# The second product of a two-layer mixture's last two token sets by Strassen's algorithm, its weights' forms made during the first layer

## Chip, cores and metric

The kernel runs on one core of a Trainium2 chip. The metric is the device time of one execution in microseconds: a median of runs, and one execution with a hardware profile. TensorE (PE) multiplies, VectorE (DVE), ScalarE (ACT) and GpSimd (POOL) do the rest, and SyncE (SP) issues the DMAs.

## The reference

Three parts in fp32, one after the other (2304 tokens, D = 512):

```python
q_s = softmax(q, over head_dim); k_s = softmax(k, over seq)
x = q_s @ (k_s.T @ v)                        # linear attention, 4 batches x 8 heads
h = x @ w_in                                 # 512 -> 2048
x = (h * clip(h + 3, 0, 6) / 6) @ w_out      # 2048 -> 512
p = domain_probs / sum(domain_probs)
for e in range(4):                           # experts, F = 1024 each
    out += p[:, e] * (relu(x @ w1[e]) @ w2[e])
```

## The kernel before

All matrices are kept as two parts, hi and lo, in the format fp32r, and each product is three matmuls: hi x hi, hi x lo and lo x hi. A matmul has a stationary tile of 128x128, loaded by a weight load of its own, and up to 512 moving columns.

**First layer** ("steps", lines 576 to 578 and 619): tokens in six blocks of 384, the 2048 inner columns in 16 chunks. A step is one chunk of one block: 12 matmuls for h, the gate (L589 on ScalarE, L592 on VectorE, L598 on ScalarE, then the low half on VectorE or GpSimd), and 12 matmuls of the second product into four PSUM banks. `PASSES1` lists which chunks run over which blocks in one pass; at the end of each pass the banks of a block are added into `acc` (L657 to L661). The weights come as 64-bit words and are unpacked on VectorE and ScalarE (L524 to L544) one chunk after another.

**Second layer** ("units", here sets): three sets of 768 tokens. Within a set the 4 x 1024 inner columns are 16 pairs of 256 columns, and two pairs are a group; `UNITS`, `NPR`, `GROUP`. The first product of a pair is a 2x2 block product (token halves, inner halves, contraction halves) by Strassen's algorithm in Winograd's form: seven products instead of eight, in the order 1, 7, 5, 6, 4, 3, 2, each 6 matmuls of 384 columns (L847). The x forms (`x_forms`) are made once a set, from sums of token and contraction blocks; the weights' forms (`w_first`) in the first set, and stored to a DRAM scratch `wd`, from which the later sets read them (L742). After the products, additions out of PSUM (L294) give the four blocks of h; `finish` applies relu and splits them into hi and lo: L924 on ScalarE, L931 on VectorE. The second product (`y_ops`, L969) is plain: for each of six token tiles and both pairs, 6 matmuls of 512 columns, whose stationary side is h; VectorE multiplies the sum by the token's share p and adds it to `acc` (L1007). Its weights are split in the first set, stored to `vd` and read back by the later sets (L798).

TensorE's order is fixed by the program: the products of one group alternate with the second-product tiles of the group before it (`tail`). For the other engines a list scheduler (`Plan.order`) sets the order ahead of time from costs written in `dve`, `act`, `pool_`, `pe` and `hop`, from due times worked back from TensorE's, and from "places": numbered buffers that an operation takes and gives back (w: weight tiles, g: tiles of h, t: temporaries, x: x forms, raw2, wtmp, xt: staging). `rather_pool` and `either` let the planner choose between GpSimd and VectorE. Each engine, SyncE too, then runs its own list strictly in order.

## Time and profile before

| | us |
|---|---|
| median of 3 runs (1259.03 to 1263.07) | 1261.53 |
| the profiled execution | 1259.79 |
| its span, first to last instruction | 1257.8 |
| TensorE busy in it | 1220.6 (97%) |
| attention and first layer, up to | about 498 |
| first set of the second layer, up to | about 742 |

The span leaves out what lies before the first and behind the last instruction. TensorE's recorded matmuls overlap, so the time that one of them takes of the engine is read from the distance of their starts and not from their durations. An engine's idle time is given with what ended it.

### The profile page before, as it was taken

The numbers are of one execution on the slowest core, as the hardware profiler recorded it, in microseconds if no ns is written. First come the engines' busy times: TensorE is split into PE (matmuls) and PEld (weight loads), VectorE is DVE, ScalarE is ACT, GpSimd is POOL, SyncE is SP. The second block draws the span as 40 slices with busy tenths as digits, with TensorE's granted clock in tenths as the row PEclk, the third lists the DMA queues.
The fourth block names the chain that finished last, engine by engine and source line by source line (L and its number), as shares of the span: only waits on it lengthen the run. The fifth ranks groups of instructions, "written<-read, shape, count | busy, mean of one in ns | idle before, by whom it ended". The sixth has DMA issues, their size and how long they took to land.

```text
span 1257.8 us, 17479 instructions
## 1 busy us (share of the span) xinstructions
PE 1220.6 (97%) x6432; PEld 1128.2 (90%) x6432; DVE 690.4 (55%) x1149; ACT 489.2 (39%) x985; POOL 334.2 (27%) x328
## 2 busy tenths in 40 slices
PE   4889999999999999999999999999999999999998
PEld 3678999999999999988888888888888888888887
DVE  8889641686365634655555684444444544444443
ACT  5667432553244334544444432222222322222221
POOL 5656222431015104667776710000000000000000
PEclk8889999999999999999999999999999999999999
DMA  8343200222013004787777656555555665555551
GB/s 290 109 147 127 68 17 1 65 70 68 1 35 109 1 1 156 270 285 252 251 251 251 226 193 209 184 184 184 184 186 185 216 205 186 185 184 184 185 167 51
DMA packets 99909, 192.59 MB, mean 153 GB/s; under 512 B 11249, under 2 KB 11249, under 8 KB 99825
## 3 DMA queue, kind: packets, MB, share of 16 engines
q1 hardware_dynamic: 99824, 191.49, 45.7%
q8 instruction: 51, 0.84, 0.3%
q14 instruction: 34, 0.27, 0.1%
HBM read 140.59 MB, written 50.86 MB: 152 GB/s over the span
## 4 chain that ended last, share of the span: by engine, by line
PE 87%; DVE 7%; issue 2%; POOL 1%; DMA 1%; ACT 0%; SPq 0%; DVEq 0%; POOLq 0%; ACTq 0%
PE ps L969 31%; PE ps L847 27%; PE ps L619 14%; PE ps L576 4%; PE ps L578 4%; PE ps L577 4%; DVE x L294 1%; PE ps L378 1%; DVE st L530 1%; PE ps L472 1%; DMA vs<-in_v_dram 1%; DMA qs<-in_q_dram 1%; PE ps L433 1%; DVE g L931 1%; DVE g L294 0%
## 5 line engine op out<-in xcount | busy, mean ns | idle before, releaser
L969 PE MATMUL ps<-w,g 128*128 128x512 f32 x1728 | 446.3, 394 | 2.5 <-ACT g L924 2.5
L847 PE MATMUL ps<-x,w 128*128 128x384 f32 x2016 | 396.5, 335 | 0.0
L847 PEld LDWEIGHTS ps<-x,w 128*128 128x128 f32 x2016 | 359.5, 188 | 25.2
L969 PEld LDWEIGHTS ps<-w,g 128*128 128x128 f32 x1728 | 320.4, 188 | 54.0 <-ACT g L924 3.0
L619 PE MATMUL ps<-g,w 128*128 128x384 f32 x1152 | 224.2, 340 | 5.7 <-ACT g L598 5.7
L294 POOL TENSOR_TENSOR w<-st,w 128x256 fp32r<-128x256 f32 (+1 forms) x160 | 155.4, 992 | 209.9 <-ACT w L544 87.6
L619 PEld LDWEIGHTS ps<-g,w 128*128 128x128 f32 x1152 | 201.7, 189 | 8.9 <-ACT g L598 6.7
L924 ACT ACTIVATE g<-t 128x384 fp32r<-128x384 f32 x192 | 100.8, 525 | 230.6 <-DVE t L294 224.0
L1007 DVE SCALAR_TENSOR_TENSOR acc<-ps,pt,acc 128x512 f32<-128x512 f32 x126 | 94.6, 751 | 167.0 <-PE ps L969 166.9
L855 ACT ACTIVATE t<-ps 128x384 f32<-128x384 f32 x192 | 94.3, 492 | 233.9 <-PE ps L847 233.9
L931 DVE SCALAR_TENSOR_TENSOR g<-t,g 128x384 fp32r<-128x384 f32 x192 | 124.2, 648 | 64.2 <-ACT g L924 64.1
L576 PE MATMUL ps<-x,w 128*128 128x384 f32 x384 | 130.5, 340 | 0.0
L577 PE MATMUL ps<-x,w 128*128 128x384 f32 x384 | 129.3, 337 | 1.1 <-DVE x L479 1.1
L578 PE MATMUL ps<-x,w 128*128 128x384 f32 x384 | 129.0, 336 | 0.0
L592 DVE SCALAR_TENSOR_TENSOR r<-r,ps 128x384 f32<-128x384 f32 x96 | 53.0, 552 | 127.9 <-ACT r L589 127.3
L589 ACT ACTIVATE r<-ps,three 128x384 f32<-128x384 f32 x96 | 55.6, 579 | 143.2 <-PE ps L578 143.2
L294 DVE TENSOR_TENSOR t<-ps,t 128x384 f32<-128x384 f32 x144 | 79.7, 554 | 40.7 <-PE ps L847 38.0
L294 DVE TENSOR_TENSOR t<-t 128x384 f32<-128x384 f32 x94 | 57.3, 610 | 70.6 <-ACT t L855 70.2
L577 PEld LDWEIGHTS ps<-x,w 128*128 128x128 f32 x384 | 72.7, 189 | 2.1 <-DVE x L479 2.0
L576 PEld LDWEIGHTS ps<-x,w 128*128 128x128 f32 x384 | 72.7, 189 | 0.8 <-ACT x L475 0.5
L578 PEld LDWEIGHTS ps<-x,w 128*128 128x128 f32 x384 | 72.7, 189 | 0.0
L598 ACT ACTIVATE g<-r 128x384 fp32r<-128x384 f32 x96 | 50.3, 524 | 52.5 <-DVE r L592 52.1
(104 smaller groups left out, 834.5 us busy)
## 6 DMA issues: line engine op xcount, KB each, us to landing
w<-wd SPq DMA_DIRECT2D x224, 256.0 KB, 4.3
w<-vd SPq DMA_DIRECT2D x128, 256.0 KB, 2.8
wd<-w SPq DMA_DIRECT2D x112, 256.0 KB, 2.5
st<-in_w_dram SPq DMA_DIRECT2D x64, 256.0 KB, 3.6
vd<-w SPq DMA_DIRECT2D x64, 256.0 KB, 3.9
st<-in_w_dram SPq DMA_DIRECT2D x30, 512.0 KB, 3.7
out_dram<-acc SPq DMA_DIRECT2D x18, 256.0 KB, 2.0
vs<-in_v_dram SPq DMA_DIRECT2D x12, 322.5 KB, 4.1
```

The lines of the kernel that those rows point to most:

```text
L294: on(o).tensor_tensor(out=out, in0=a, in1=b, op=op)
L576: nc.tensor.matmul(pst[0], lhsT=hi, rhs=a, start=(k == 0), stop=False)
L577: nc.tensor.matmul(pst[0], lhsT=hi, rhs=b, start=False, stop=False)
L578: nc.tensor.matmul(pst[0], lhsT=lo, rhs=a, start=False, stop=(k == NK - 1))
L589: nc.scalar.activation(out=pst["r"], in_=pst[0], func=AF.Relu, bias=three)
L619: nc.tensor.matmul(y, lhsT=l, rhs=r, start=(s["start"] and not low and m == 0), stop=(s["stop"] and bool(low)))
L847: nc.tensor.matmul(bank(i), lhsT=l, rhs=r, start=(opens and k == 0 and m == 0), stop=(k == 1 and m == 2), skip_group_check=not opens)
L855: nc.scalar.activation(out=t, in_=bank(i), func=AF.Copy)
L924: nc.scalar.activation(out=g[:, :n], in_=x(), func=AF.Relu)
L931: nc.vector.scalar_tensor_tensor(out=g[:, n:2 * n], in0=x(), scalar=0.0, in1=g[:, :n].bitcast(F32), op0=ALU.max, op1=ALU.subtract)
L969: nc.tensor.matmul(y, lhsT=l, rhs=rr, start=opens and x == 0, stop=closes and x == len(seq) - 1)
L1007: o1 = add({"DVE": dve(DM) + 0.05}, lambda o: nc.vector.scalar_tensor_tensor(out=a, in0=state[ti], scalar=s, in1=a, op0=ALU.mult, op1=ALU. ...
```

## The change

In the last two sets the second product becomes a Strassen product too: inner halves of a pair by output halves of 256 columns by token halves. Its left side (h) needs seven forms per pair, of which four are sums; relu stands before them, so h's blocks are first finished (`relu`, and two-operand steps with a maximum) and then summed: s1, n2, s3, s4. Each of the seven products is 6 matmuls of 256 columns for each of three token tiles and the two pairs of a group together. Products 1, 6, 7 and 4 of a tile add up in the same PSUM region, 5 and 3 in another, 2 stands alone; after each, VectorE multiplies the region by p and adds it into the block of `acc` that Winograd's scheme needs (`INTO`).

The weights' seven forms for it (`w_prepare(pr, 1)`, all 16 pairs) are made during the first layer, after the attention's memory is free, and stored to `vd`; the places for that are taken from w, g and t of the first layer. A pass more is made in the first layer. The first set keeps the plain second product (`h_ops0`, `y_ops0`, `w_second0`), and no longer stores its halves. The later sets read seven forms per pair instead of four halves. x places are lent to h and t, and one staging buffer to h. The planner's costs change: VectorE operations between SBUF tiles, GpSimd, and the way to and from SyncE.

```diff
-PASSES1 = [(0, 3, range(3)), (3, 6, range(3)), (0, 6, range(3, 6)), (6, 11, range(6)),
-           (11, 16, range(6))]
+PASSES1 = [(0, 3, range(3)), (3, 6, range(3)), (0, 6, range(3, 6)), (6, 9, range(6)), (9, 13, range(6)), (13, 16, range(6))]
...
-BLOCKS = [(0,), (1,), (2,)]
...
+ORDER2 = (5, 2, 1, 6, 3, 7, 4)
+CHAIN = {5: "x", 3: "x", 2: "b", 1: "a", 6: "a", 7: "a", 4: "a"}
+BANK2 = {"x": ((0, 0), (0, 256), (1, 0)), "b": ((2, 0), (2, 256), (1, 256)),
+         "a": ((3, 0), (3, 256), (2, 0))}
+INTO = {5: (1, 1), 2: (0, 0), 1: (0, 0), 6: (0, 1), 3: (0, 1), 7: (1, 1), 4: (1, 0)}
...
-MORE_W, MORE_G, MORE_T = 2, 4, 5
-NX, NXG = 24, 4
+MORE_W, MORE_G, MORE_T = 2, 4, 3
+RING, WAIT = 2, 2
+NX, NXG = 24, 7
...
-    return 0.27 if b == "PE" else 0.2 if a == "PE" else 1.05 if a == "SP" else 0.16
+    if b == "SP":
+        return 2.0
+    return 0.27 if b == "PE" else 0.2 if a == "PE" else 2.5 if a == "SP" else 0.16
...
+def dve2(n):
+    return 0.155 + 1.6e-3 * n
...
-    return 0.15 + 2.25e-3 * n
+    return 0.2 + 2.4e-3 * n
...
-    vd = dram.tile([NPR, 2, 2, P, DM], F32, name="vd")
+    vd = dram.tile([NPR, 7, P, DM], F32, name="vd")
...
-    XT = [s[:, 768 * i:768 * (i + 1)] for s in ST for i in range(2)]
+    XT = [ST[0][:, 768 * i:768 * (i + 1)] for i in range(2)]
...
+    def w_prepare(pr, second):
...
+        p0, p1 = [raw2(2 * pr + f) for f in range(2)]
...
+            o = temps[i] = load("wtmp", rather_pool(half), make, ready[a] + ready[b], ("wtmp", None))
...
+        def form(i):
+            pl = w_new(store, (pr, i, second), "wr")
+            t = (pr, i, second)
+            o1 = add({"ACT": act(half)}, lambda o: nc.scalar.activation(
+                out=store[t][:, :half], in_=vals[i](), func=AF.Copy), ready[i] + [pl])
+            give = [("wtmp", temps[i])] if i in temps else []
+            o2 = add(rather_pool(half), lambda o: half_sub(
+                o, store[t][:, half:], vals[i](), store[t][:, :half]),
+                [o1] + (readers[i] if i in temps else []), None, give)
+            w_stored[t] = add({"SP": 0.9}, lambda o: nc.sync.dma_start(
+                out=(vd if second else wd)[pr, i - 1], in_=store[t].bitcast(F32)), [o2], None,
+                [("wr", pl)])
+            all_.append(o2)
...
+        form(1)
+        if second:
+            summed(7, 0, 3, ALU.subtract)
+        else:
+        form(7)
+        summed(5, 0, 1, ALU.subtract)
+        summed(6, 5, 3, ALU.subtract)
+        form(5)
+        summed(4, 2, 6, ALU.add)
+        form(6)
+        form(4)
+        form(3)
+        form(2)
+        stage2.append(add({"": 0.0}, lambda o: None, all_, None, [("raw2", p0), ("raw2", p1)]))
...
+    def w_bring(pr, second, i):
+        store, kept = (w2, vd) if second else (w1, wd)
+        pl = w_new(store, (pr, i))
+        return load("sp", {"SP": 0.9}, lambda o: nc.sync.dma_start(
+            out=store[pr, i].bitcast(F32), in_=kept[pr, i - 1]), [pl, w_stored[pr, i, second]]), pl
...
-        sts = []
-        for x, o in enumerate((o1, o2)):
-            sts.append(add({"SP": 0.9}, lambda o, x=x: nc.sync.dma_start(
-                out=vd[pr, f, x], in_=w2[pr, f, x].bitcast(F32)), [o]))
-            w_stored[pr, "v", f, x] = sts[-1]
-        stage2.append(o2)
-        return [o1, o2], pls, sts
...
-    def h_ops(pr, u, weights, last):
+    def h_ops(pr, u):
...
+        def relu(src, dep):
+            return add({"ACT": act(n)}, lambda o: nc.scalar.activation(
+                out=at(src), in_=at(src), func=AF.Relu), [dep])
...
+        def form(i, src, deps, raw, free):
...
+            o2 = add({"DVE": dve2(n)} if raw else rather_pool(n), low,
+                     [o1] + (free or []), None, [] if free is None else [("t", src)])
...
+        def make(i):
+            ld, pl = w_bring(pr, 0, i)
+            deps = [ld, xf["op", (u, i)]] + bank_free.get(BANK[i], [])
+            give = [("w", pl)]
+            if pr == NPR - 1:
+                give += [("x", pl) for pl in x_place[u, i]]
+            ops[i] = main_pe(6 * pe(n), lambda o: product(o, i), deps, None, give)
+            if i in (1, 7, 5, 6):
+                pos[i] = evict(i)
+                bank_free[BANK[i]] = [pos[i]]
+            if i == 6:
+                y0, p5, uu = pos[7], pos[5], pos[6]
+                s = add(rather_pool(n), lambda o: tt(o, at(y0), at(y0), at(p5), ALU.add), [y0, p5],
+                        None, [("t", p5)])
+                c22 = pos["c22"] = add(rather_pool(n), lambda o: tt(
+                    o, at(y0), at(y0), at(uu), ALU.add), [s, uu])
+                pos["r22"] = relu(y0, c22)
+            if i == 4:
+                uu, y0 = pos[6], pos[7]
+                c = pos["c21"] = tmp({"DVE": dve(n)}, lambda o, t: tt(
+                    o, t, bank(4), at(uu), ALU.add), [ops[4], uu])
+                bank_free[1] = [c]
+                s1 = pos["s1"] = tmp({"DVE": dve2(n)}, lambda o, t: nc.vector.scalar_tensor_tensor(
+                    out=t, in0=at(c), scalar=0.0, in1=at(y0), op0=ALU.max, op1=ALU.add),
+                    [c, pos["r22"]])
+                form(4, y0, [pos["r22"]], False, [s1])
+            if i == 3:
+                uu = pos[6]
+                c = pos["c12"] = tmp({"DVE": dve(n)}, lambda o, t: tt(
+                    o, t, bank(3), at(uu), ALU.add), [ops[3], uu])
+                bank_free[2] = [c]
+                add({"": 0.0}, lambda o: None, [c, pos["c21"], pos["c22"]], None, [("t", uu)])
+                form(5, pos["s1"], [pos["s1"]], False, None)
+                pos["l2"] = form(2, c, [c], True, None)
+            if i == 2:
+                a0, c21, c12, s1 = pos[1], pos["c21"], pos["c12"], pos["s1"]
+                c11 = add({"DVE": dve(n)}, lambda o: tt(o, at(a0), bank(2), at(a0), ALU.add),
+                          [ops[2], a0])
+                bank_free[3] = [c11]
+                r11 = relu(a0, c11)
+                n2 = tmp(either(n), lambda o, t: tt(o, t, at(a0), at(s1), ALU.subtract), [r11, s1])
+                s3 = add({"DVE": dve2(n)}, lambda o: nc.vector.scalar_tensor_tensor(
+                    out=at(c21), in0=at(c21), scalar=0.0, in1=at(a0), op0=ALU.max,
+                    op1=ALU.subtract), [r11, s1])
+                s4 = add({"DVE": dve2(n)}, lambda o: nc.vector.scalar_tensor_tensor(
+                    out=at(c12), in0=at(c12), scalar=0.0, in1=at(n2), op0=ALU.max, op1=ALU.add),
+                    [n2, pos["l2"], made[2][1]])
+                add({"": 0.0}, lambda o: None, [n2, made[5][2]], None, [("t", s1)])
+                form(1, a0, [r11], False, [n2, s3])
+                form(6, n2, [n2], False, [s4])
+                form(3, c12, [s4], False, [])
+                form(7, c21, [s3], False, [])
...
+    def y_ops(u, prs, gs, step):
...
+        def part(i, t):
...
+                opens = i in (5, 2, 1)
...
+                for pi, pr in enumerate(prs):
+                    g, ww = gs[pi][i][0], w2[pr, i]
+                    hi, lo = g[:, :n][:, c], g[:, n:2 * n][:, c]
+                    seq += [(hi, ww[:, :half]), (hi, ww[:, half:]), (lo, ww[:, :half])]
+                for x, (l, r) in enumerate(seq):
+                    nc.tensor.matmul(y, lhsT=l, rhs=r, start=clears and x == 0,
+                                     stop=x == len(seq) - 1, skip_group_check=True)
...
+                if t == 0:
+                    weights[i] = [w_bring(pr, 1, i) for pr in prs]
...
+                if i in (5, 2, 1):
+                    deps += bank2_free.get(b, []) if at == 0 else []
+                else:
+                    deps += dep[key]
+                o = main_pe(6 * pe(half), fn, deps)
+                if t == n // P - 1:
+                    o.give += [("g", gs[pi][i][3]) for pi in range(len(prs))]
+                    o.give += [("w", pl) for _, pl in weights[i]]
+                dep[key] = [evict(i, t, o)]
...
+            y = PS[4 + b][:, at:at + half]
...
+            if fresh:
+                o1 = add({"DVE": dve(half)}, lambda o: nc.vector.tensor_scalar_mul(a, y, s),
+                         [made] + norm + x_read[u, hf])
+            else:
+                o1 = add({"DVE": dve(half) + 0.03}, lambda o: nc.vector.scalar_tensor_tensor(
+                    out=a, in0=y, scalar=s, in1=a, op0=ALU.mult, op1=ALU.add), [made])
+            o1.due = made.due + made.eng["PE"] + 1.5
...
+        return [part(i, t) for i in ORDER2 for t in range(n // P)]
...
-        [("w", NW + i) for i in range(MORE_W)] + [("g", NG + i) for i in range(MORE_G)]
+        [("wr", NW + i) for i in range(MORE_W)] + [("raw2", NG + i) for i in range(MORE_G)]
+        + [("wtmp", i) for i in range(3)]
         + [("t", NT_ + i) for i in range(MORE_T)] + [("ph", 2), ("ph", 3)])
...
+    for pr in range(NPR):
+        w_prepare(pr, 1)
...
+    add({"": 0.0}, lambda o: None, stage2, None, [("g", NG + i) for i in range(MORE_G)])
+    ring = [o for s, o in zip(steps, products) if s["c"] == PASSES1[-2][0]][:1]
+    for i in range(RING):
+        o = add({"": 0.0}, lambda o: None, ring, ("w", None), (), 0.0)
+        o.give.append(("wr", o))
+    for i in range(MORE_W + RING):
+        o = add({"": 0.0}, lambda o: None, stage2, ("wr", None), (), 0.0)
+        o.give.append(("w", o))
...
-        o = load("xg", {"": 0.0}, lambda o: None, [evicted[NK - 1]], ("x", None))
+        o = load("xg", {"": 0.0}, lambda o: None, [evicted[NK - 1]], ("x", None), 0.0)
         o.give.append(("g", lambda o=o: 100 + o.place))
+    load("xg", {"": 0.0}, t_of_x, (), ("x", None), 0.0).give += [("t", 100), ("t", 101)]
...
+            slots = GROUP * len(ORDER) - WAIT
+            count = len(tail)
+            for x, pr in enumerate(group):
+                make, gs[x] = h_ops(pr, u)
+                for z, i in enumerate(ORDER):
+                    make(i)
+                    slot = x * len(ORDER) + z - WAIT + 1
+                    while slot > 0 and count - len(tail) < -(-count * slot // slots):
+                        tail.pop(0)()
...
+            tail += y_ops(u, group, gs, step)
+        if u == 0:
+            add({"": 0.0}, lambda o: None, stage0, None, [("xt", i) for i in range(2)])
+            add({"": 0.0}, g_of_stage, stage0, None, [("g", 200), ("g", 201)])
...
```

## Rows read from the trace of the kernel before

**Rows 1.** The page, part 1: span, and TensorE's busy time (instructions).

```profile
span 1257.8 us, 17479 instructions
...
PE 1220.6 (97%) x6432; PEld 1128.2 (90%) x6432; DVE 690.4 (55%) x1149; ACT 489.2 (39%) x985; POOL 334.2 (27%) x328
```

**Rows 2.** Busy time by stretch: length, each engine's us; granted clock, DMA share, GB/s.

```profile
core 0: us, PE busy (x) PEld busy (x) DVE busy (x) ACT busy (x) POOL busy (x), PEclk, DMA share, GB/s
165.00:491.30 326.30, 323.49 (x1865) 322.78 (x1864) 170.01 (x283) 130.29 (x238) 78.95 (x70) 1.00 0.12 40
541.80:741.80 200.00, 198.30 (x990) 177.98 (x988) 120.65 (x164) 96.10 (x207) 136.38 (x147) 1.00 0.71 248
...
930.40:961.70 31.30, 31.30 (x158) 28.13 (x157) 14.12 (x25) 8.14 (x16) 0.00 (x0) 1.00 0.58 187
```

**Rows 3.** Timeline of TensorE, second set: start, us, engine, line, tiles, shape, count.

```profile
900.97 1.55 PE L969 MATMUL ps<-w,g 128*128 128x512 f32 x6
902.36 1.21 PE L847 MATMUL ps<-x,w 128*128 128x384 f32 x6
903.41 1.55 PE L969 MATMUL ps<-w,g 128*128 128x512 f32 x6
```

**Rows 4.** Timelines in the attention: weight loads (PEld), and matmuls with 129 columns.

```profile
52.06 0.19 PEld L619 LDWEIGHTS ps<-g,w 128*128 128x128 f32 x1
...
52.06 0.30 PEld L619 LDWEIGHTS ps<-g,w 128*128 128x128 f32 x2
...
57.59 1.27 PE L378 MATMUL ps<-vs,acc 128*128 128x129 f32 x10
58.70 1.28 PE L378 MATMUL ps<-spare,acc 128*128 128x129 f32 x10
```

**Rows 5.** Groups by shape, VectorE, 830 to 1200: busy us, mean ns, idle before.

```profile
L931 DVE SCALAR_TENSOR_TENSOR g<-t,g 128x384 fp32r<-128x384 f32 x96 | 53.3, 555 | 34.4 <-ACT g L924 34.3
L1007 DVE SCALAR_TENSOR_TENSOR acc<-ps,pt,acc 128x512 f32<-128x512 f32 x65 | 48.8, 751 | 92.0 <-PE ps L969 92.0
L294 DVE TENSOR_TENSOR t<-ps,t 128x384 f32<-128x384 f32 x72 | 40.0, 555 | 26.2 <-PE ps L847 24.7
```

**Rows 6.** Groups by shape, VectorE, 500 to 700, where GpSimd works too.

```profile
L931 DVE SCALAR_TENSOR_TENSOR g<-t,g 128x384 fp32r<-128x384 f32 x53 | 42.5, 804 | 16.2 <-ACT g L924 16.2
```

**Rows 7.** Groups by shape, VectorE, 170 to 400: an eviction of 384 columns.

```profile
L661 DVE SCALAR_TENSOR_TENSOR acc<-ps,acc 128x384 f32<-128x384 f32 x32 | 15.6, 548 | 2.3 <-PE ps L619 2.3
```

**Rows 8.** Groups by shape, GpSimd, whole span: operations of 256 and 384 columns.

```profile
L294 POOL TENSOR_TENSOR w<-st,w 128x256 fp32r<-128x256 f32 x112 | 89.4, 826 | 91.5 <-PE ps L619 58.4 <-ACT w L764 32.6 <-DVE g L931 0.5
...
L294 POOL TENSOR_TENSOR g<-r,g 128x384 fp32r<-128x384 f32 x25 | 28.0, 1122 | 57.7 <-ACT g L598 51.3 <-PE ps L619 6.4
...
L294 POOL TENSOR_TENSOR t<-t 128x384 f32<-128x384 f32 x2 | 3.0, 1502 | 250.2 <-ACT t L855 248.7 <-DVE t L294 1.4
```

**Rows 9.** Groups by shape, ScalarE, 830 to 1200.

```profile
L924 ACT ACTIVATE g<-t 128x384 fp32r<-128x384 f32 x95 | 49.9, 525 | 136.9 <-DVE t L294 136.1 <-POOL t L294 0.8
L855 ACT ACTIVATE t<-ps 128x384 f32<-128x384 f32 x94 | 46.3, 492 | 134.8 <-PE ps L847 134.8
```

**Rows 10.** Timeline of TensorE where the second set begins.

```profile
742.56 2.08 PE L969 MATMUL ps<-w,g 128*128 128x512 f32 x6 [2.46 <-ACT g L924]
744.43 2.12 PE L847 MATMUL ps<-x,w 128*128 128x384 f32 x6
746.36 2.18 PE L969 MATMUL ps<-w,g 128*128 128x512 f32 x6
```

**Rows 11.** Groups by shape, VectorE, 700 to 745: forms of the next set.

```profile
L294 DVE TENSOR_TENSOR x<-acc,x 128x768 fp32r<-128x768 f32 x4 | 5.1, 1270 | 0.0
```

**Rows 12.** Waits of TensorE, 165 to 495: total us, times, longest.

```profile
PE ps L619 <- ACT g L598: 2.8, 2, 1.5
```

**Rows 13.** DMA issues: count, KB each, median us to landing.

```profile
w<-wd SPq DMA_DIRECT2D x224, 256.0 KB, 4.3
```

**Rows 14.** Timeline of TensorE at the end of the span.

```profile
1241.58 12.53 PE L969 MATMUL ps<-w,g 128*128 128x512 f32 x54
```

More of the change, by code (lines that the diff above doesn't have):

```diff
@@ L280, in queue, with load @@
         return in_turn.setdefault(name, [])
-    def load(name, eng, fn, deps=(), take=None):
-        o = add(eng, fn, queue(name) + list(deps), take)
+    def load(name, eng, fn, deps=(), take=None, key=None):
+        o = add(eng, fn, queue(name) + list(deps), take, (), key)
         in_turn[name] = [o]
@@ L493, in half_sub, with w_new @@
         tt(o, out, x, hi.bitcast(F32), ALU.subtract)
-    def w_new(store, key, deps=()):
+    def w_new(store, key, kind="w"):
         def new(o):
             store[key] = w_tile(o.place, "w_" + "_".join(str(x) for x in key))
-        return load("w", {"": 0.0}, new, deps, ("w", None))
+        return load(kind, {"": 0.0}, new, (), (kind, None))
     w0, w_done, w_place = {}, {}, {}
@@ L583, in h_part @@
         h_before[:] = [o0]
+        products.append(o0)
         if s["x_last"]:
@@ L704, in x_forms @@
             key = u, i
-            pls = x_place[key] = [load("form", {"": 0.0}, lambda o: None, rdy, ("x", None))
+            pls = x_place[key] = [load(
+                "form", {"": 0.0}, lambda o: None, rdy + (queue("xg") if u else []), ("x", None))
                                   for _ in range(2)]
@@ new lines, in tile_kernel, with raw0 @@
+    w1, w2 = {}, {}
+    def w_bring(pr, second, i):
[3 more added lines that the diff above has]
+            out=store[pr, i].bitcast(F32), in_=kept[pr, i - 1]), [pl, w_stored[pr, i, second]]), pl
+    w2_0 = {}
+    stage0 = []
+    def raw0(c, i):
+        ld = load("raw0", {"SP": 0.95}, lambda o: nc.sync.dma_start(
+            out=RAW2[o.place], in_=w[c][:, i * DM:(i + 1) * DM]), (), ("raw0", None))
@@ L828, in h_ops, with h_ops0 @@
+    last0 = []
+    def h_ops0(pr, u, weights, last):
         n = UNITS[u][1]
@@ L977, in emit @@
                     deps.append(o1 if low == 0 else o2)
-                if step["last"] and closes:
-                    for pr2 in prs:
-                        for f in range(2):
-                            deps += seconds[pr2, f][2]
                 o = main_pe(cnt * pe(DM), fn, deps, ("y", None) if opens else None)
@@ L1061, in tile_kernel @@
         h_part(i, s)
-    for b in range(NK):
-        add({"": 0.0}, lambda o: None, [evicted[b]], None, [("y", b)])
     for i in range(4):
         bank_free[i] = list(last1)
+        add({"": 0.0}, lambda o: None, [evicted[i]], None, [("y", i)])
+    for pr in range(NPR):
[5 more added lines that the diff above has]
+        o.give.append(("wr", o))
@@ L1073, in tile_kernel, with t_of_x, g_of_stage @@
         o.give.append(("g", lambda o=o: 100 + o.place))
-    weights, seconds = {}, {}
+    def t_of_x(o):
+        t = xp.tile([P, 768], F32, tag=f"x{o.place}", name="tx")
+        t_more[100], t_more[101] = t[:, :384], t[:, 384:]
+    load("xg", {"": 0.0}, t_of_x, (), ("x", None), 0.0).give += [("t", 100), ("t", 101)]
+    def g_of_stage(o):
+        t = wsp.tile([P, 3 * DM], F32R, tag="st1", name="gs")
+        g_more[200], g_more[201] = t[:, :768], t[:, 768:]
     tail = []
-    for blk, units in enumerate(BLOCKS):
+    for u in range(len(UNITS)):
@@ L1077, in tile_kernel @@
         for g0 in range(0, NPR, GROUP):
             group = list(range(g0, g0 + GROUP))
-            for pr in group:
-                weights[pr] = w_first(blk, pr)
-            for pr in group:
-                for f in range(2):
-                    seconds[pr, f] = w_second(blk, pr, f)
-            for u in units:
-                step = dict(first=g0 == 0, final=g0 + GROUP >= NPR, last=u == units[-1], e=g0 // NPE)
-                gs = [None, None]
-                early, late_ = y_ops(u, group, gs, seconds, step)
+            step = dict(first=g0 == 0, final=g0 + GROUP >= NPR, last=True, e=g0 // NPE)
@@ L1088, in tile_kernel @@
+            gs = [None] * GROUP
+            if u == 0:
+                firsts0 = [w_first0(pr) for pr in group]
+                seconds0 = {(pr, f): w_second0(pr, f) for pr in group for f in range(2)}
+                early, late_ = y_ops0(u, group, gs, seconds0, step)
                 for x, pr in enumerate(group):
-                    make, gs[x] = h_ops(pr, u, weights[pr], step["last"])
+                    make, gs[x] = h_ops0(pr, u, firsts0[x], True)
                     for z, i in enumerate(ORDER):
@@ L1098, in tile_kernel @@
                 tail += late_
-        if blk == 0:
-            add({"": 0.0}, lambda o: None, stage2, None, [("xt", i) for i in range(4)])
-        if blk < 2:
-            x_forms(blk + 1)
+                continue
+            slots = GROUP * len(ORDER) - WAIT
[7 more added lines that the diff above has]
+                        tail.pop(0)()
+            if not bank2_free:
+                for i in range(4):
+                    bank2_free[i] = list(last0)
+            tail += y_ops(u, group, gs, step)
+        if u == 0:
+            add({"": 0.0}, lambda o: None, stage0, None, [("xt", i) for i in range(2)])
+            add({"": 0.0}, g_of_stage, stage0, None, [("g", 200), ("g", 201)])
+        if u + 1 < len(UNITS):
+            x_forms(u + 1)
     for f in tail:
```

190 lines of the change are left out of this document (148 added, 42 removed).

## The prediction, made before the change was run

> **What bounds the kernel now.** I read the page's busy line first, then the busy time by stage, then single instructions of TensorE. TensorE is busy 97% of the span [rows 1]. By stage the reader is to see that it is the bound in every one: in the first layer (165 to 491.3 us) it loses 2.8 of 326.3 us, in the first set of the second layer (541.8 to 741.8) 1.7 of 200, and in the last two sets nothing: one group of two pairs takes 31.3 us, all of it busy, while VectorE has 14.1 and ScalarE 8.1 us of work and GpSimd none [rows 2]. So a TensorE instruction taken out of the last two sets is worth its whole spacing, as long as no other engine fills up.
>
> The spacing is read from starts, since recorded durations overlap. Six 512-column matmuls lie between 900.97 and 902.36, 1.39 us, and six of 384 columns between 902.36 and 903.41, 1.05 us [rows 3]: 0.231 and 0.175 us each. A group has 84 of the second kind (14 products of 6) and 72 of the first (6 token tiles x 2 pairs x 2 chunks x 3): 14.65 + 16.65 = 31.3 us, which is the stretch above. The account closes, so the sum below is made with these.
>
> **The second product.** 72 matmuls of 512 columns become 126 of 256 (7 forms x 3 token tiles x 6). That is 7/8 of the columns, but 54 more instructions. No fp32r matmul here has 256 columns. From below: half of the 512-column one, 0.116 us; from above: the line through 384 and 512 columns, 0.231 - 2 x 0.056 = 0.119. I take 0.117, so 14.75 us instead of 16.65: 1.9 us per group, with ends 1.65 and 2.05. Sets two and three have 8 groups each: **16 x 1.9 = 30 us** (26 to 33).
>
> This holds only while the next stationary tile is loaded behind a running matmul. Every matmul has its own load, recorded as 188 ns, more than 117. But at 52.06, where TensorE starts anew, the first load is recorded as 0.19 us and two together as 0.30, so the second starts 0.11 after the first; and in the attention, ten 129-column records with a load each take 1.11 us (57.59 to 58.70), 0.111 apiece [rows 4]. A load thus goes through in 0.11 us, just under the 0.117 that it must hide behind. The margin is thin, and that is the first rival. The Trainium skill (TensorE: Matmul & The Clock Gate, Part 3, The mechanism) says that a weight load overlaps running matmuls only in another row group; by that rule the 54 further loads of a group would each show. The trace speaks against it: 384 columns at 2.4 GHz are 0.16 us, and a shown load would make the spacing 0.27, not 0.175.
>
> **The other engines in the last two sets.** Per pair VectorE gets three additions out of PSUM at 0.555 us [rows 5], four two-operand steps between SBUF tiles and one more subtraction, which took 0.555 with GpSimd idle [rows 5] and 0.804 with it at work [rows 6]; I take 0.8, since GpSimd will work: 5.7 us, 11.4 per group. It also gets 21 evictions of 256 columns instead of 6 of 512 at 0.751 [rows 5]. At 384 columns from PSUM one took 0.548 [rows 7]; the line through both gives 0.35 at 256, and 0.548 itself is the other end. I take 0.45: 9.5 us (7 to 11.5). Together 21 of 29.4 us, 71%. The two sums for the block C22 and six low halves per pair may go to GpSimd, 16 per group at 1.12, 1.5 where VectorE competes [rows 8]: 18 to 24 us. ScalarE has 8 evictions at 0.492 and 18 steps at 0.525 [rows 9]: 13.4 us. None is full. TensorE runs in a fixed order, so what counts is whether a result comes before its turn: a group's forms are wanted only after three more products (3.1 us). The tight chain is another: tiles 1, 6, 7, 4 add up in one PSUM bank, so each must be evicted before the next is added. Between a tile's turn in 1 and in 6 lie two other tiles and at least one product, 2 x 0.70 + 1.05 = 2.45 us; drain, eviction and restart are about 0.9 (twice the eviction, an estimate), and 1.5 us are left for waiting behind another VectorE instruction of at most 1.3. In the first set's stretch, with VectorE at 60% and GpSimd at 68%, TensorE lost 1.7 in 200 us [rows 2]; at that rate the 470 us cost **+4** (0 to 10).
>
> DMA: 28 loads per group instead of 22. 187 GB/s at a share of 0.58 becomes about 252 GB/s; the first set moves 248 at 0.71 with TensorE full [rows 2]. A load lands in 4.3 us [rows 13], and 26 places hold nearly a group in advance. Nothing on the path. If that cover went, each late tile would cost up to those 4.3 us.
>
> **The first layer.** Prepared there: 16 pairs x (4 sums + 7 low halves) = 176 operations of 256 columns at 0.826 on GpSimd [rows 8], 145 us, on top of 79 of 326: 69%, what the first set has now. ScalarE gets 112 short copies, on 130 of 326 us. SyncE gets 32 loads and 112 stores; a store waits there for its low half, and the loads of the first layer's own weights stand behind it, though these run a chunk or more ahead. One pass more means 24 more evictions of 0.55 on VectorE (13 us on 170 [rows 2]). VectorE's gating step feeds TensorE here and gets slower beside a busy GpSimd. Today's waits in this layer are 2.8 us [rows 12]. Ends: -2.8 if they go, +16 if it crowds (second rival). I take **+2**. The first set's stores of the plain halves (64) fall away on SyncE, where nothing on the path waited for them: 0.
>
> The new planner costs (landing 2.5 instead of 1.05 us, VectorE and GpSimd dearer) reorder everything, the attention included. Nearer to the durations above, they might take a wait away as well as make one: **0**, from -4 to +4.
>
> **Borders.** Between sets one and two TensorE waits 2.46 us for ScalarE's g tile [rows 10]; the wait is behind VectorE, which was making the next set's x forms at 1.27 us each without a pause [rows 11]. After it six 384-column matmuls take 1.93 us, 0.32 each: the lower clock level, 1.2 GHz. Wait and slow clock cost some 4.4 us. The change leaves 16 x places instead of 20 for two sets that need 14 each, and two scratch tiles instead of four, so most forms wait for a product of the set's last pair; but they still have about seven products (15 us) each. It also costs the planner's forms more truly. Ends per border: -4.4 and +4.4; I take **0** in sum. At the end, 54 matmuls run after the last product with no gap [rows 14]; afterwards 21 tiles run there, the first of which need the forms of the last pair: **+1** (0 to 3).
>
> **Sum.** -30 + 4 + 2 + 0 + 0 + 1 = -23 us. The profiled execution took 1259.79 us, 2 us over its span, and lies 1.7 us under the median of 1261.53. 1259.8 - 23 = 1236.8 there; against the median, 1238.5.
>
> **Rivals.**
> 1. The load is the bound. If loads came only every 0.188 us, as recorded, a group's second product would take 126 x 0.188 = 23.7 us, 7 more than now: 16 x 7 = +113, 1374 us. It decides from a spacing of 16.65 / 126 = 0.132 on. Against it: 0.11 in [rows 4]; for it: that the trace shows no fp32r matmul under 384 columns. Chance 0.03. In a second form the load shows at every matmul that is added: 54 x 0.11 [rows 4] - 1.9 = 4 us a group, +64, 1327; it needs a spacing that 384 columns don't have [rows 3]. Chance 0.02. The skill's rule above is this form.
> 2. The preparation crowds the first layer: if each of some 78 steps (24 matmuls, 4.2 us) after 165 us waits 0.2 us longer, 16 us go, 1254. For it: gate and low half share VectorE with evictions; against: two PSUM places more let products run ahead. 0.12.
> 3. It ends slower because VectorE becomes the bound of sets two and three. If GpSimd's 16 operations fall to VectorE at 0.8 [rows 6], it has 21 + 12.8 = 33.8 us a group, 2.5 over the 31.3 of now: 16 x 2.5 = +40, 1302. It decides where VectorE's work passes 31.3 us a group. For it: GpSimd is slow and the planner gives VectorE what GpSimd can't start in time; against: GpSimd idles there now. 0.07.
> 4. It does not do what it says: the planned order does not fit the real times, waits in the chain of four take about 1.4 us a group, and all is eaten: 1261. 0.08.
>
> **How the numbers follow.** The forecast, with its own ends 1222 to 1252, gets 0.68. Low end: 33 us, no waits, first layer's waits gone. High end: 26 us, 10 for waits in groups, a few in the first layer. The range goes on to 1258, to take in rival 2. A measurement tells about 0.3% (4 us) from no change. Faster: 0.68 + 0.12 = 0.80; same 0.08; slower 0.05 + 0.07 = 0.12.
>
> **What would show it.** In the changed kernel's timeline six 256-column matmuls should start 0.70 us apart, and a group should take 29.4 to 29.8 us with TensorE busy throughout; VectorE should be at 70 to 80% there and GpSimd above 50%. The first layer should end where it ends now, within 4 us. Wrong would be: spacing above 0.132, TensorE waits on the evictions of the second product, long waits for the gate in the first layer, or several us at both borders.

## The result and the profile after

The changed kernel takes 1242.59 us (median of 4 runs, 1241.78 to 1242.94), the kernel before 1260.28 in the runs beside it: a ratio of 0.9857, 95% interval 0.9835 to 0.9879, 17.7 us less. The forecast was 1238.5 us and 23 us less, with a range from 1222 to 1258. The profiled execution, the slowest of the four, has a span of 1241.2 us, 16.6 under that of before.

The page's first part, and the busy time by stretch (length, each engine's us, granted clock, DMA share, GB/s), as [rows 1] and [rows 2] have them for before:

```profile
PE 1200.1 (97%) x7296; PEld 1151.6 (93%) x7296; DVE 877.5 (71%) x1482; ACT 595.4 (48%) x1257; POOL 665.4 (54%) x659
...
164.00:507.00 343.00, 339.49 (x1935) 334.48 (x1934) 225.26 (x343) 170.24 (x361) 209.70 (x225) 1.00 0.45 154
541.80:741.80 200.00, 200.00 (x999) 179.88 (x998) 124.58 (x187) 96.40 (x214) 115.02 (x124) 1.00 0.54 185
858.20:887.90 29.70, 29.70 (x211) 29.52 (x210) 21.78 (x41) 12.69 (x27) 13.79 (x13) 1.00 0.79 249
```

The reader is to see that TensorE is still the bound, that a group now takes 29.7 us instead of 31.3, and that it is paid for with VectorE (14.1 to 21.8 us a group) and GpSimd (0 to 13.8). TensorE's timeline in a group (start, us, line, shape, count), beside [rows 3]:

```profile
845.66 1.21 PE L933 MATMUL ps<-x,w 128*128 128x384 f32 x6
846.71 1.59 PE L1249 MATMUL ps<-w,g 128*128 128x256 f32 x12
848.14 1.21 PE L933 MATMUL ps<-x,w 128*128 128x384 f32 x6
849.18 0.87 PE L1249 MATMUL ps<-w,g 128*128 128x256 f32 x6
849.89 0.52 PE L1249 MATMUL ps<-w,gs 128*128 128x256 f32 x3
```

Twelve matmuls of 256 columns lie between 846.71 and 848.14: 0.119 us each.

Where the 16.6 us come from, by the starts of the last matmul of the first layer and of the first product of the second set in the two timelines:

| stage | before | after | difference |
|---|---|---|---|
| attention and first layer end | 498.6 | 507.0 | +8.4 |
| first set | 239.2 | 239.3 | +0.1 |
| second and third set, to the end of the span | 520.0 | 494.9 | -25.1 |

The -25.1 are 16 x (16.64 - 14.96) = -26.9 of matmuls, -4.6 at the border of sets one and two, and about +6 of new waits: 0.13 us once in most groups, 1.9 at the border of sets two and three, 1.8 at the end. The border now (as [rows 10]) and the end of the span (as [rows 14]), TensorE's timeline:

```profile
746.30 3.29 PE L933 MATMUL ps<-x,w 128*128 128x384 f32 x18
749.42 1.55 PE L1176 MATMUL ps<-w,g 128*128 128x512 f32 x6
...
1224.26 0.98 PE L1249 MATMUL ps<-w,g 128*128 128x256 f32 x6 [0.43 <-DVE acc L1298]
...
1227.65 6.73 PE L1249 MATMUL ps<-w,g 128*128 128x256 f32 x54 [0.25 <-DVE acc L1298]
1234.63 2.42 PE L1249 MATMUL ps<-w,g 128*128 128x256 f32 x18 [0.26 <-DVE acc L1298]
```

No wait is left where set two begins. The listed waits for `acc` have one thing in common, which is read by counting the matmuls and the evictions from the start of set two: TensorE waits for the eviction of the *other* tile in the same PSUM bank (`BANK2` puts two tiles of 256 columns into a bank). At the end these are the third tile of product 2 behind the third of 5, the first of 6 behind the second of 1, and the first of 4 behind the second of 7. So it is not the chain in which the prediction looked for waits, where a tile waits for its own eviction, but one with a tile less between. The 0.13 us in most groups are of this kind too. The wait is listed for the weight load, here before product 4:

```profile
797.38 1.09 DVE L998 SCALAR_TENSOR_TENSOR t<-t,tx 128x384 f32<-128x384 f32 x1
798.39 0.86 DVE L1298 SCALAR_TENSOR_TENSOR acc<-ps,pt,acc 128x256 f32<-128x256 f32 x2
798.91 0.77 PEld L1249 LDWEIGHTS ps<-w,g 128*128 128x128 f32 x6 [0.19 <-DVE acc L1298]
```

The eviction of 7's second tile stands behind a step between SBUF tiles of 1.09 us, ends at 798.86, and the load starts 0.05 us later.

VectorE and GpSimd in the last two sets (groups by shape, 800 to 1200: busy us, mean ns, idle before), beside [rows 5, 8]:

```profile
L1298 DVE SCALAR_TENSOR_TENSOR acc<-ps,pt,acc 128x256 f32<-128x256 f32 x265 | 122.4, 480 | 66.4 <-PE ps L1249 64.5
L310 DVE TENSOR_TENSOR t<-ps,t 128x384 f32<-128x384 f32 x51 | 28.2, 552 | 9.5 <-PE ps L933 8.6 <-ACT t L946 0.7
L1020 DVE SCALAR_TENSOR_TENSOR t<-t 128x384 f32<-128x384 f32 x14 | 13.7, 979 | 0.0
L965 DVE SCALAR_TENSOR_TENSOR g<-t,g 128x384 fp32r<-128x384 f32 x19 | 10.5, 554 | 0.0
...
L310 POOL TENSOR_TENSOR g<-t,g 128x384 fp32r<-128x384 f32 x82 | 90.6, 1110 | 103.5 <-ACT g L956 101.2 <-PE ps L1249 1.2 <-PE ps L933 1.1
```

An eviction of 256 columns takes 0.48 us (reckoned 0.45). Operations that read PSUM keep their time, 0.552; those between SBUF tiles take from 0.55 to 1.0 (reckoned 0.8).

### The profile page after: what moved, and what is told of

The parts are those of the page before. It is cut to its first block, busy times and chain, and to the rows that moved or that the text cites. A ratio compares the mean times of both kernels' runs of the same rounds, so it can differ in the third digit from the quotient of the medians.

```text
span 1241.2 us, 21145 instructions
## 1 busy us (share of the span) xinstructions
PE 1200.1 (97%) x7296; PEld 1151.6 (93%) x7296; DVE 877.5 (71%) x1482; ACT 595.4 (48%) x1257; POOL 665.4 (54%) x659
## 4 chain that ended last, share of the span: by engine, by line
PE 83%; DVE 7%; POOL 3%; issue 3%; DMA 2%; ACT 1%; SPq 0%; POOLq 0%; DVEq 0%; ACTq 0%
PE ps L1249 19%; PE ps L933 18%; PE ps L642 11%; PE ps L1176 11%; PE ps L1054 9%; PE ps L598 4%; PE ps L600 4%; PE ps L599 4%; POOL w L310 1%; PE ps L400 1%; DMA vd<-w 1%; PE ps L494 1%; POOL st L310 1%; POOL g L310 1%; DVE x L310 1%
## 5 line engine op out<-in xcount | busy, mean ns | idle before, releaser
L1249 PE MATMUL ps<-w,g 128*128 128x256 f32 x1737 | 244.4, 283 | 2.0 <-DVE acc L1298 1.8
L1249 PEld LDWEIGHTS ps<-w,g 128*128 128x128 f32 x1737 | 228.6, 190 | 6.0 <-DVE acc L1298 6.0
L933 PEld LDWEIGHTS ps<-x,w 128*128 128x128 f32 x1344 | 227.3, 189 | 0.8
L1298 DVE SCALAR_TENSOR_TENSOR acc<-ps,pt,acc 128x256 f32<-128x256 f32 x312 | 143.4, 480 | 79.6 <-PE ps L1249 77.6
L310 POOL TENSOR_TENSOR w<-st,w 128x256 fp32r<-128x256 f32 (+1 forms) x129 | 130.7, 1027 | 103.9 <-ACT w L891 70.2
L310 POOL TENSOR_TENSOR g<-t,g 128x384 fp32r<-128x384 f32 x98 | 107.6, 1104 | 116.6 <-ACT g L956 114.4
L1176 PE MATMUL ps<-w,g 128*128 128x512 f32 x576 | 148.9, 394 | 0.0
L1054 PEld LDWEIGHTS ps<-x,w 128*128 128x128 f32 x672 | 119.4, 188 | 7.8
L1176 PEld LDWEIGHTS ps<-w,g 128*128 128x128 f32 x576 | 106.8, 188 | 16.5
L956 ACT ACTIVATE g<-t 128x384 fp32r<-128x384 f32 x145 | 73.8, 521 | 43.0 <-DVE t L998 18.0
L310 POOL TENSOR_TENSOR st<-st 128x256 f32<-128x256 f32 (+1 forms) x66 | 71.0, 1081 | 34.2 <-DVE st L561 32.8
L941 ACT ACTIVATE t<-ps 128x384 f32<-128x384 f32 x90 | 44.1, 490 | 70.1 <-PE ps L933 69.9
L599 PEld LDWEIGHTS ps<-x,w 128*128 128x128 f32 x384 | 72.7, 189 | 3.1 <-DVE x L501 3.0
```

What stands on the lines that cost most here:

```text
L310: on(o).tensor_tensor(out=out, in0=a, in1=b, op=op)
L599: nc.tensor.matmul(pst[0], lhsT=hi, rhs=b, start=False, stop=False)
L933: nc.tensor.matmul(bank(i), lhsT=l, rhs=r, start=(opens and k == 0 and m == 0), stop=(k == 1 and m == 2), skip_group_check=not opens)
L956: nc.scalar.activation(out=made[i][0][:, :n], in_=at(src), func=AF.Relu if raw else AF.Copy)
L1054: nc.tensor.matmul(bank(i), lhsT=l, rhs=r, start=(opens and k == 0 and m == 0), stop=(k == 1 and m == 2), skip_group_check=not opens)
L1176: nc.tensor.matmul(y, lhsT=l, rhs=rr, start=opens and x == 0, stop=closes and x == len(seq) - 1)
```

## The experiments

Two theories were held against rivals: that the matmul's spacing is set by its columns down to the time of a weight load, and that the 8.4 us lost before the first set come from the preparation and from the planner's costs. "First layer's waits" below is the sum over TensorE's matmuls, from the end of the attention to that of the first layer, of the spacing over 0.174 us: 2.5 us before, 6.5 after. The waits that a view lists are less (3.1 of the 6.5), since a load that shows behind a wait, or a slow clock, is not among them.

How far single profiles agree can be read from the runs themselves. The first set takes 239.3 us in every run, and what follows it 494.4 to 495.4 in every run of the changed kernel whose last two sets are the same, so these runs differ in where the first layer ends. Three runs change only the last two sets ("fewer columns" and the two without GpSimd), and their engines run the same instructions in the same order up to there as the changed kernel. They end the first layer at 506.0, 504.5 and 504.8 us with waits of 5.3 to 5.7, where the changed kernel's profile has 507.0 and 6.5. So the +8.4 are +5.9 to +8.4, and a difference of 2.5 us between two profiles is not to be read.

**Fewer columns.**

```diff
+                cols = {5: 128, 3: 192, 2: 224}.get(i, half)
-                seq += [(hi, ww[:, :half]), (hi, ww[:, half:]), (lo, ww[:, :half])]
+                seq += [(hi, ww[:, :cols]), (hi, ww[:, half:half + cols]), (lo, ww[:, :cols])]
```

> The changed kernel with fewer moving columns in three of the seven products of the second product: 128 in 5, 192 in 3, 224 in 2, and 256 in the others (these products leave out the rest of their columns). If each matmul has to wait for its weight load of about 0.11 us, the three are spaced 0.109 to 0.112 us apart whatever their columns, a group saves 54 x 0.009 = 0.5 us, and the whole takes about 1235 us. Rival: the columns alone set the spacing; then 0.105, 0.090 and 0.060 us, 1.8 us less a group, about 1213 us.

One run, 1237.0 us. TensorE's timeline:

```profile
851.51 0.47 PE L1250 MATMUL ps<-w,gs 128*128 128x192 f32 x3
851.82 1.23 PE L1250 MATMUL ps<-w,g 128*128 128x192 f32 x9
852.89 1.23 PE L933 MATMUL ps<-x,w 128*128 128x384 f32 x6
...
863.51 0.50 PE L1250 MATMUL ps<-w,gs 128*128 128x128 f32 x3
863.85 0.50 PE L1250 MATMUL ps<-w,g 128*128 128x128 f32 x3
...
868.00 0.50 PE L1250 MATMUL ps<-w,gs 128*128 128x224 f32 x3
868.34 0.50 PE L1250 MATMUL ps<-w,g 128*128 128x224 f32 x3
```

Three of 128 columns take 0.34 us (863.51 to 863.85), three of 224 also 0.34 (868.00 to 868.34), twelve of 192 take 1.38 (851.51 to 852.89): 0.113 to 0.115 apiece, where columns alone would give 0.060, 0.105 and 0.090. The medians of the three are 0.111, 0.112 and 0.111. That is the weight load of [rows 4], seen from the other side. A fixed time for every matmul, whatever its load, is not the reason: in the attention of the changed kernel four loads of 64 rows take 0.32 us, where two of 128 took 0.30 [rows 4], and the four matmuls with them start 0.06 us apart:

```profile
125.21 0.32 PEld L455 LDWEIGHTS ps<-ident,spare 64*128 64x128 f32 x4 [0.25 <-issue]
125.21 0.46 PE L455 MATMUL ps<-ident,spare 64*128 64x64 f32 x4
```

So 256 columns are 0.008 us above the floor, and a second halving would have gained hardly anything per matmul.

**The planner's costs undone.**

```diff
-    if b == "SP":
-        return 2.0
-    ... else 2.5 if a == "SP" else 0.16
+    ... else 1.05 if a == "SP" else 0.16
-    return 0.155 + 1.6e-3 * n
+    return 0.155 + 1.05e-3 * n
-    return 0.2 + 2.4e-3 * n
+    return 0.15 + 2.25e-3 * n
```

> The changed kernel with the planner's old costs (landing 1.05 us, old VectorE and GpSimd costs), nothing else undone. If the new costs made the attention 4.4 us longer and took away the wait between sets one and two, then the last TensorE instruction of the attention comes back to about 159.7 us (now 164.1), the wait of some 2.5 us and the slow clock behind it return at the start of set two (about 4.4 us), and the total stays within 2 us of 1242.6. Rival: the moved buffers made both; then the attention still ends at 164 and no wait returns at the border.

1256.2 us (ratio to before 0.9959, 0.9945 to 0.9974). A miss: the attention does end earlier, at 160.8 (159.7 foretold), but the first layer's waits rise from 6.5 to 22.6 us, and the border stays without a wait. The costs are not a side matter: without them three quarters of the gain are gone. TensorE's waits in the first layer (total us, times, longest; line numbers are two less than in the changed kernel):

```profile
PE ps L640 <- ACT g L619: 11.2, 10, 2.1
PE ps L640 <- DVE g L308: 3.8, 6, 1.3
```

In the changed kernel these are 2.0 and 1.1. Only the way to and from SyncE undone (the first part of the diff):

> The changed kernel with the planner's old way to and from SyncE (landing 1.05 us, no 2 us ahead of a store), and the new VectorE and GpSimd costs. With all costs old, TensorE waited 22.6 us in the first layer. If the engine costs make the difference, it waits about 6.5 us here and the attention ends at 160.8: 1239 us. If the landing time does, it waits 15 us or more: 1250 or more.

1251.6 us (0.9935, 0.9915 to 0.9955), first layer's waits 20.8. So most of these waits, and 9.0 of the 13.6 us, go with the way to and from SyncE; the rest goes with the engines' costs. How it reaches TensorE is seen on ScalarE. It makes the high halves of the preparation (L791, here L789), each of which needs a place that a store to `vd` gives back, and in the same list the gate. ScalarE's waits for these stores, first in the changed kernel and then in this run, and one of them in this run's timelines:

```profile
ACT w L791 <- DMA vd<-w: 1.8, 3, 0.8
...
ACT w L789 <- DMA vd<-w: 44.3, 41, 3.8
...
315.26 0.42 ACT L789 ACTIVATE w<-raw 128x256 fp32r<-128x256 f32 x1 [3.81 <-DMA vd<-w]
315.58 0.51 ACT L619 ACTIVATE g<-r 128x384 fp32r<-128x384 f32 x1
...
316.14 1.15 PE L640 MATMUL ps<-g,w 128*128 128x384 f32 x5 [1.15 <-ACT g L619]
```

With the short landing time the planner counts on a place whose store is not done (median 2.2 us from issue to landing in this run), ScalarE stands in its fixed list, and the gate stands behind it. How much of the 20.8 us comes this way was not added up.

**The costs alone**, in the kernel before (the same diff, the other way round):

> The kernel before with the new planner costs alone. If the costs act by themselves: attention ends at about 164 us instead of 159.7, the 2.5 us wait at the start of set two goes, total within 2 us of 1260.3. Rival (buffers, not costs): attention ends at 159.7, the wait stays, total the same.

1268.9 us, slower than before (1.0057, 1.0037 to 1.0076). The attention ends at 164.2 as expected, the first layer at 504.9 instead of 498.6, as late as in some runs of the changed kernel; the wait at the border does not go but grows to 4.8 us. The wait was expected to go, so this half is a miss. The same costs that the changed kernel needs harm the old one.

**The landing time of the attention's loads alone.**

```diff
+                    lands = 1.05 if o.take and o.take[0] in ("kt", "v", "q") else self.after(e, x)
-                    x.at = max(x.at, o.end + self.after(e, x))
+                    x.at = max(x.at, o.end + lands)
```

> The changed kernel in which the planner takes the old landing time (1.05 us) for the loads of the attention alone (k, v, q). If the longer landing time there makes the attention's order worse, the attention ends at about 160.8 us instead of 164.1 and the total is about 1239. Rival: the order is changed by the other costs or by the weights' loads; then 164 and 1242.6 stay.

1238.0 us (0.9824, 0.9805 to 0.9843), 4.6 less than the changed kernel, as expected, but not where: the attention's last instruction comes at 166.6, later than before, while the first layer ends at 503.4 instead of 507.0. First-layer steps run between the attention's instructions (18 more matmuls than in the changed kernel lie before it), so the attention's end does not measure what was lost there; the first layer's end does. Most of the gain shows behind the attention, where the waits fall from 6.5 to 3.6 us; it is not only an order within the attention. This is the fastest of the kernels that compute the whole; the two intervals overlap, the runs don't (1237.5 to 1239.3 against 1241.8 to 1242.9). Yet most of these loads take 3.3 to 3.6 us to land in the changed kernel (medians of the three largest groups), so the truer cost gave the worse order here.

**The preparation made light.**

```diff
-            o = temps[i] = load("wtmp", rather_pool(half), make, ...)
+            vals[i], ready[i] = vals[a], ready[a]
-            o1 = add({"ACT": act(half)}, ...high half...)
-            o2 = add(rather_pool(half), ...low half...)
+            o2 = add({"ACT": act(DM)}, lambda o: nc.scalar.activation(
+                out=store[t], in_=p0.place_tile[:, :DM], func=AF.Copy), ready[i] + [pl])
```

> The changed kernel with the 176 sums and low halves left out of the preparation in the first layer: ScalarE copies one raw tile into each form, loads and stores stay (the forms are not the right ones). If GpSimd and VectorE work of the preparation makes TensorE wait in the first layer, its waits between 165 and 507 us fall from about 7 us to 3 or less, the first layer ends at about 503 us and the whole takes about 1238.5. Rival: the waits come from the added pass and the unpacking of the first layer's weights, and stay: 1242.

1236.7 us (0.9804, 0.9788 to 0.9819). The first layer's waits fall to 1.4, and it ends at 501.7. By the medians the work of the preparation costs 5.9 us; by the first layer's end it is 5.3 against the changed kernel's profile and 2.8 against the earliest with the same order. The end of the attention stays (163.9).

**The preparation on GpSimd only** (`rather_pool(half)` becomes `{"Pool": pool_(half)}` in `w_prepare`).

> The changed kernel with all 176 sums and low halves of the preparation bound to GpSimd (VectorE has 18 of those of the first layer, 17.5 us). If VectorE's own share delays the gate, TensorE's waits in the first layer fall from 6.5 to about 3 us: 1239. Rival: the waits come from VectorE's other instructions being slower while GpSimd works (0.63 to 0.71 us for the low half, 0.46 to 0.74 for the unpacking's shift); then they stay at 5 to 8 us: 1242 to 1244.

1240.2 us (0.9842, 0.982 to 0.9863). The waits are 4.8 us, between the two cases; of the 3.2 us by which the first layer ends sooner (503.8), 1.4 show at the attention's end already, which the edit does not touch. Both numbers lie just under those of the runs with the changed kernel's own order (504.5 to 507.0, waits 5.3 to 6.5), so a gain is not shown beyond their spread, and VectorE's own share of the preparation explains a small part at most. That the rest goes with GpSimd's work beside VectorE is argued, not shown; the light preparation took both away at once. With the attention's landing time as well:

> The changed kernel with both: old landing time for the attention's loads, and the preparation's sums and low halves on GpSimd alone. If the two gains are of different places (4.6 and 2.4 us), they add up: the first layer ends at about 501 us and the total is about 1236. Rival: both only shift the same waits, and the total is 1238 or more.

1239.0 us (0.9826, 0.9812 to 0.9839): no better than the landing time alone, so the gains do not add up in the median. In the profile the first layer does end at 502.0, near the 501 expected and 1.4 us before that of the landing time alone, which is within what profiles differ by.

**The old passes** (`(6, 11, range(6)), (11, 16, range(6))`).

> The changed kernel with the first layer's old passes (chunks 6 to 10 and 11 to 15 instead of three passes). Theory: the passes only make room for the weight tiles of the preparation; with longer passes fewer weight tiles are free, chunks are unpacked in a rush at the pass borders, and TensorE's waits in the first layer (6.5 us now) grow to 9 or more: 1245 us or more. Rival: the added pass with its 24 evictions is what costs; then the waits fall to about 4 us: 1240.

1279.7 us (1.0154, 1.0125 to 1.0183): slower than before the change. The direction was right and the size far off: the first layer's waits grow to 43 us. Of these 27.7 are listed as waits, 22 of them for the weights themselves; the granted clock is 0.95 in the mean from 164 to 543 us, 1.00 in the changed kernel's first layer. TensorE's waits from 164 to 543 us, the largest:

```profile
PE ps L642 <- ACT w L566: 8.5, 2, 5.8
PE ps L642 <- ACT g L621: 5.0, 5, 1.8
PE ps L598 <- ACT w L566: 4.5, 2, 2.7
PE ps L642 <- DVE w L310: 4.2, 2, 2.6
```

The added pass looks like a cost (24 evictions) and is what keeps the preparation's lending of weight places from becoming a loss of 37 us.

**Fewer x places in the kernel before** (`NX, NXG = 24, 8`).

> The kernel before with four more x places lent to h, so that 16 are left for the x forms, as in the changed kernel. If too many early x forms made the wait at the border of sets one and two, it falls from 2.5 us to under 0.5, the slow clock behind it goes, and the total is about 1256. Rival (the tile order of the changed kernel, three products ahead of the first tile, took the wait away): it stays, 1260.

1257.5 us (0.9964, 0.9949 to 0.9979). Where TensorE waited 2.46 us [rows 10], it now waits 0.2, and the slow clock behind it is gone (0.50 of full speed was granted from 744.3 to 747.7 us before, 1.00 here; six matmuls of 384 columns again take 1.05 us):

```profile
737.91 2.25 PE L847 MATMUL ps<-x,w 128*128 128x384 f32 x12
740.00 1.08 PE L969 MATMUL ps<-w,g 128*128 128x512 f32 x4
741.26 0.72 PE L969 MATMUL ps<-w,g 128*128 128x512 f32 x2 [0.18 <-DVE g L931]
741.83 1.21 PE L847 MATMUL ps<-x,w 128*128 128x384 f32 x6
742.88 1.55 PE L969 MATMUL ps<-w,g 128*128 128x512 f32 x6
```

With more free places VectorE makes forms for the next set early, ahead of halves that TensorE wants now; with fewer they are spread. The other runs agree: with the old costs and the new places the border has no wait, with the new costs and the old places it has 4.8 us.

**No GpSimd in the last two sets** (`rather_pool(n)` and `either(n)` become `{"DVE": dve2(n)}` in `h_ops`).

> The changed kernel with all sums and low halves of the last two sets on VectorE, none on GpSimd. The prediction's rival 3 put 16 more operations at 0.8 us on 21 us: 33.8 us a group, against 29.7 now, so 16 x 4.1 = +66, about 1308 us. Other theory: VectorE's operations between SBUF tiles are slow (0.8 to 1.1 us) only because GpSimd works beside it; alone they take 0.555, a group has 2 x (3 x 0.55 + 5 x 0.56) + 21 x 0.48 + 16 x 0.56 = 28 us, still under 29.7, and the kernel takes 1243 to 1252 us with VectorE at 90% or more.

1274.3 us (1.0102, 1.0081 to 1.0123): slower than before, and neither theory holds. VectorE's operations do fall to 0.55 us, but it is busy only 80%, while TensorE waits. A group of VectorE operations between SBUF tiles (1030 to 1190), TensorE's waits from 507 us on, and the busy time from 800 to 1000:

```profile
L310 DVE TENSOR_TENSOR g<-t,g 128x384 fp32r<-128x384 f32 x43 | 23.0, 550 | 0.0
...
PE ps L933 <- DVE t L310: 18.5, 7, 4.7
PE ps L1249 <- DVE acc L1298: 4.4, 5, 2.5
...
800.00:1000.00 200.00, 183.32 (x1268) 180.81 (x1266) 159.54 (x328) 79.25 (x164) 11.86 (x6) 0.98 0.72 226
```

The planner reckoned 0.77 for each of these. With 0.56 (`dve2(n)` becomes `dve(n)` there):

> As the run without GpSimd in the last two sets, but the planner reckons these VectorE operations at 0.56 us (as they took there, 0.55) instead of 0.77. That run took 1274 us with VectorE at 80% and TensorE waiting 30 us for additions out of PSUM that stood behind low halves in VectorE's list. If the wrong cost made that list, the waits fall below 8 us and the kernel takes 1242 to 1248 us. If VectorE's load itself makes them, it stays at 1268 or more.

1245.6 us (0.9879, 0.985 to 0.9908), and over the same stretch:

```profile
800.00:1000.00 200.00, 196.06 (x1368) 195.20 (x1367) 167.37 (x350) 86.73 (x176) 6.41 (x3) 0.98 0.76 240
```

VectorE has more work there, 84%, and TensorE waits less. In a group it now has 24.7 us of work. The load was not the trouble; the order made from a wrong cost was.

## Why the prediction held, point by point

**The sum.** -25 us were forecast for the last two sets with their border and end (-30 + 4 + 0 + 1), -25.1 were measured. That they agree so well is luck: inside, three terms were off and cancelled. The spacing was taken as 0.117 and is 0.119, the upper end of its bounds: -26.9 instead of -30. The border was put at 0, from -4.4 to +4.4, and gave the whole -4.6; the reason was found in the places (fewer x places lessen the burst), and the prediction had read the same cut as a danger. Waits in the groups and at the second border were about 4 us, as taken, the end 1.8 instead of 1; but the waits come from the neighbour in the bank and not from a tile's own eviction. The mechanism of the gain itself held: a group took 29.7 us, with VectorE at 73% of it. GpSimd had 46%, not above 50%: 13 operations at 1.0 to 1.1 us, where 16 at up to 1.5 had been reckoned.

**The terms that failed** are the first layer and the new costs: +2 and 0 forecast, +8.4 measured in the profile (5.9 at least), against the prediction's own sign that the first layer ends within 4 us of now. The same matmuls lie between the end of the attention and that of the first layer before and after (343 us now, 339 then), so the +8.4 split into +4.4 up to the end of the attention and +4.0 of waits behind it. The first part goes with the costs, which were put at 0, from -4 to +4: the old kernel with them ends the attention at 164.2, the changed one at 162.7 to 164.1 in its order and at 160.8 without them. The second part goes with the preparation's work, since the waits fall from 6.5 to 1.4 us without it; the second rival describes it, at a quarter to a third of its price. The two are not independent: the landing time in the attention, worth 4.6 us by its own run, takes waits away behind the attention as well. The prediction reckoned GpSimd's load (69%; measured 209.7 of 343, 61%) and named the slower gate without a price for it; VectorE was busy 66% of that stretch.

**The costs that seemed to be bookkeeping** were put at -4 to +4. With the new buffers they are worth 13.6 us (1256.2 against 1242.6), with the old ones they cost 8.4 (1268.9 against 1260.5).

**The first rival** (the load is the bound) was decided rightly, and by the right rows: 0.111 in [rows 4], 0.111 in the run with fewer columns. In its second form, loads that show at every matmul, it stands against the spacing of 0.119; the rule of the Trainium skill named in the prediction is not what this trace shows.

**The third rival** (VectorE becomes the bound) did not come in the changed kernel: 21.8 us a group were measured, 21 reckoned. Its price was wrong, since it took VectorE's slow time with GpSimd at work for a case without GpSimd: alone, VectorE carries all of it at 1245.6 us, with 24.7 us a group instead of 33.8. Yet a kernel of this family does end slower than before, by the planned order (1274.3).

## What to carry to other kernels

Before more and smaller matmuls are traded for fewer columns, find the spacing at which weight loads come through: here 0.111 us, so a matmul of 256 columns is still paid by its columns, and one of 224 costs as much as one of 128. In a kernel whose order is planned ahead, a change's buffers and the planner's costs are part of the change: the same operations took from 1238.0 to 1279.7 us here with other places, passes and costs, and the costs deserve runs of their own. A cost taken from another state can be dear (0.77 us for 0.55: 29 us), but a truer cost is no promise of a better order: the long landing time was worth 9 us here in all, and lost 4.6 at the attention's loads. Tiles that share a PSUM bank should be planned together, since here one waited for the other's eviction. Added work on idle engines should be priced in the stage where it is put, by what it delays there, and not by whether it fits.

## What the runs showed of the hardware

VectorE operations between SBUF tiles took 0.55 us with GpSimd idle and up to 1.0 us with it at work, for the same 384 columns, while those that read PSUM stayed at 0.55; the spread within one stretch (0.554 and 0.979 in the rows above) is wider than the 0.8 that was reckoned for all. The Trainium skill (GPSIMD Engine Reference, Specifications) says that GpSimd shares its way to SBUF with VectorE and contends with VectorE's instructions that have two SBUF inputs; these runs agree in that the 0.55 came back without GpSimd. Behind a wait for an eviction the second matmul starts some 0.10 us late, about one weight load of 0.11 [rows 4] that is not hidden there. A matmul into one half of a PSUM bank waited for the eviction of the other half; whether the chip or only the program's semaphores ask for that was not tried.
